# Whole 512-column units at the turn from pass 1 to pass 2 of a fused spectral and gated feed-forward kernel

## The chip, the cores and the metric

The kernel runs on one core of a Trainium2 chip. The metric is the device time of one execution in microseconds (us). Three runs of the kernel before took 1045.95 to 1046.25 us, with a median of 1046.12 us.

## The reference

Two layers, each of a spectral mixing with a residual and a feed-forward block with a residual, on x with 2048 rows and 512 columns:

```python
def _A_ref(x, w_r, w_i):                       # x: [1, 2048, 512]
    X = rfft2(x)
    X = X * (w_r + 1j * w_i)                   # [2048, 257]
    return irfft2(X, s=(2048, 512))

def _B_ref(x, w_gate, w_up, w_down):           # F = 1792
    g = einsum("bsd,df->bsf", x, w_gate)
    u = einsum("bsd,df->bsf", x, w_up)
    return einsum("bsf,fd->bsd", g * u, w_down)

for _ in range(2):
    x = x + _A_ref(_layernorm(x), w_r, w_i)
    x = x + _B_ref(_layernorm(x), w_gate, w_up, w_down)
```

All is in float32.

## The kernel before

**Layout.** The 2048 rows are 16 tiles of 128 (index t). Every layer has the transform stages (`fwd`, `middles`, `inv`) and then the feed-forward part. The feed-forward part takes F in 14 blocks of 128 features (`ft`) and runs twice over them: pass 1 for row tiles 0 to 7 (`h0 = 0`), pass 2 for tiles 8 to 15 (`h0 = 8`). Pass 1 goes through the blocks upward and pass 2 downward, so that the weights of the last blocks are still there. The place between the two passes is called the turn; there is one in each layer.

**A unit** (`unit`) computes g, u and g*u for one block of 128 features and one pass. It uses a 2 x 2 scheme with seven products instead of eight, so X is kept as seven *forms*, f0 to f6: `xA` holds f0, f1, f2 and `xS` holds f3 to f6, each as `[form, high or low, k, 512 columns]`. A form is a sum of blocks of X; its high part is a cast made by ScalarE (ACT) and its low part the difference to the full value, a subtraction made by GpSimd (POOL). A product is six matmuls (`mm3` for two k: high by high, high by low, low by high). In the order in which a unit uses them: gw on f3, gx on f1, gy on f4, gx on f2, gz on f5, gv on f6, gz on f0. A unit covers 512 columns (`half` is None), or a half unit covers 256 of them.

**The downs** bring g*u back to 512 columns. Layer 0's pass 1 does it directly (`db`, three 512-wide matmuls on tiles `wd` and `h`). The three other passes use the seven-product scheme again (`down`: `ex`, `ey`, `ew`, `ev`, `ez`, six 256-wide matmuls each), on forms `sf` of g*u, again a cast by ACT and a subtraction by POOL, and on forms `bf` of the down weights. Layer 0 makes these forms, stores them (`dn`), and loads them as `bf` for pass 2 and for layer 1. `bf` lies in the memory of `h` and `wd`, so the first of them can be loaded only behind the last `db` of pass 1.

**The second X.** `xA` and `xS` exist once. While pass 1 runs, the forms of pass 2's rows are prepared in a staged copy, the tile `xf`, `[4 row blocks r, 8 pieces, k, 128]` (`stage_x`): normalised rows are transposed through DRAM (`turns`), and POOL makes the sums. `unstage_x` (line 721) then copies them into `xA` and `xS`, for one row block r at a time: three casts by ACT (768, 512 and 512 columns) and three subtractions by POOL of the same widths. It is called for two row blocks at k = 16 of the main sequence and for the other two at k = 18. A copy must wait until the products of pass 1 that read its columns have run.

**What sets the order.** The main sequence `seq` lists the units. Around the turn it was: whole units up to block 11, then half units (12, 13, 12, 13 in pass 1; 13, 12, 13, 12 in pass 2), then whole units from block 11 down. Its index k also places the stages, the weight loads (`weights`, `kept_weights`) and the due times (`begins`). But the order of the instructions on each engine is a finished table: `Plan.order` reads `ORDER`, a compressed list of all operations of the program in the order of issue, and `PLACES`, which names the buffer of each tile. Each engine executes its instructions in that order. All are issued through one helper, so that the profile has one line for nearly all, L314 (`Queue.call`); they are told apart by the tiles' names. SyncE (SP) issues the DMAs.

Of the kernel before, what the change touches and what calls it, by code (L numbers as in the profile page):

```python
# [28 lines left out]
def consts():  # L29
# [86 lines left out]
    'c-lRh37n7B_s7qDW-&92F=mLdj2Zhr)<MaVeNBpFDYRNDm8C>zv4m2Qq<&Gf$d-MVtT7D3*mpk)5zP!^=DFwpzK{MtUcSro+~?f0e9k$abH79iit;B)ZfQ};(R*4zjAUssxvM$aPzuNa'  # L116
    '-XD@&J*Cl7LU!tda#KU(Ppu@|G)Y1wfhTkHA1%z9a;z>Xw>3t}$|a<hlw(>=3dvsNUC>0irbVQrM9F@x#>sYGlVq)?BH^CCEt~YL9?~-M2hY7GbM=JQk*jKv`nP6lAvE2`oh13MZbH`<'
    'a!4D=KkOAJH_+`U|9nlB6DHbLWX*XkA=!Ly#QsZJbynlJe^H;1^GHsVZ%j{n7dhqSH||6sqn@18)7l#At4JCv8?e_l{83mU*((;CqU4VLp*OXLT+~uX{|9{*XkWRkW#t=fj~$VC@3gj*'
    'UiuFECd&wYo-0>1A@D>jT2#ePxA4aSU95v;7W(|9t?*}zln;x`JECcL_+DU{Vo^4c31Mw7FU0QQdoirthi2#Wt`S=ec~L~A7#`LjayPZ0l*7Wx{M(@Qv7?TpYk9nWSqI>wOl+;f)5p+!'
    'mA)yv(X1R#89tT6z8G{oKwKY`m8|JQq}s|Jy^QYX^$ziAf}Eu~S|;mQaq-#7^JV3A?IBBamF&>lL^xKe$!ebI!tUF&BmOKZ(d<!@`>oL?PA2O6*q5*2_$V9Sox<;KuUJXsbAnXonO-uE'  # L120
    '7|hiX@~WN*-<f+&`%6QaLR{nVew4(6u%hy`t_E52Z3k0@?;~}tRAi^W_&ZYP5H0uZE)q}bE4n~Rf$Cha6e}+BcXfo0XHA?$fUvQ6>nmL^ZS_}auFK>XeOiu#gl2qpnGquy`jYODJniN!'
    '@Qd)iTOI-V&zWrdI~dL)I?js;nrL=wDZMOJiFpYvYNBPGz9n0bP)BBKNj)m<q^>NpSJ0{pIQ|?&wUc_}%_e(Hx|^SEJGo$+g{1p?^ny3pPvc1=Ps$f)_!)WD7lf_TDq6(cw5`p2ogs5{'
    'g;oH4ZKXdr>?yBkKVq4o=WKanvExattmTczlMA#Pk=mwT%0fNPZe64dE9Ynn*~-6CGD<hda6To;e~8Z`(nE&u-hw)CRp#4z(v&QHR?d6(@_Vt1uc7*o36%r3mT8BCwHhXcw754^U)81('
    '#+7;IE89(mT4UNsbJ;F&`n^6Ztz|4Za$RDH%#Ru>7D?gKU3!6z2~?NGVDJMpy>InK{Sj1bCF>W7hXr+AKFCz<jE6hubZM-!C5`V#L2+eJc|bQwD}4&7i$G{aDMH4$JBPI~Pv(+=A##M*'
    'AISJwGE{%ngLqA~J6d_fC=<l&(HHRFU1WvhgJ|ORv>ql#xAZH#QW34%;)!9%OC%#U>ML?kBjf>Dtk20OSh!P%@ccI2E^ksP7DyzL?_pVnyst0GcSw1Ty7CY8?hP=Lt5?yrF<JMXHs|$0'
    'RwPh$rh@(t@k2#y*$$>kn7g3AusPsYFs=p{lL5r3C4TnM@isVeahz|q+D*FEPB2@@*@L#Ec~(|n?=eaD8<|`QQ7cPBM&+H9)3yp8J*r8@w}m8EA~Z|GOg^8lkt5~gjFi`fwxJhE-tW*n'
    '`P<f&({j(om}D~co)pkO@$3V}uy&6vYS#JfyaTqO$)|pO4qC#&%VrHVp5{w^WOguXeZ{}k$=Rto9Di=r>MCZg|E{?pLXWA4{Nj3pI$&6nq6a|YaT{gwY?3K0SM;<^Hs>_gRyAkU+NNd~'
    'NchfHGV~W4XCm?W4f}{mCmW7xaV<>+z9c#J7P1;3bGbeWR`aQt*QqV>`1vCB<OV&*Ros<20klSG1UsFuC%D#KmXUL1Kwku}M$V9lE2%?2bLV#(Z?=*Pk>q3-d04)&E#-4+tI(<Hm^_`w'
    'y7Tr0JHl&4hs~!tAJd`!Chre+iUsFC+a4xSrrOud8`?kznf=5tLyuV_Pf!7jq?#u3G4I3h-WufAmf3i?HI=m{$SWuL_BlJtt10D(<`ytuWIa{*wk`oL>-8BrO9cKtL!2tmy(UW^`?z@;'
    'l#T%xe-gLFc8FQ4Ep;Uo>`Sc$#+KN>wY^!QFVj!9YgwYuMJC%(cv}3UUPrE7VTV;j?{BJ58mR3@CrJdW4}p%pGSH4OY5F*t46tL(Hgr%>U61FUk!S2eb3(_nq9YyuPd!IGE@&I_cR2|B'  # L130
    'UYk)1%gbBXJJ2{=dfO-&V^-657TO#zw#}^9_w6|Doxqb;Pm+Hz=<={s*0r*cI$cC+5TBED;j>6@DQmcv4Enm#VV3G;JJg)UYs>M@DRo@rq<&!MnLgCPM%1ULOm#ZJCOUfx{9`5^us>IS'
    '(hVk=`WQ++_r~+>>4Jx;J3Z|b6KA8nRr;+Bl?CP(n81Uwi<+|ljmjdkH#RH)e=V@>Nj{}YCHKj0HG}9Z4h_k62RVG0eBVbbhM5E@VI!$EQ%oh9Pha{5{OtE5yz1cQq^7dZCb=WeP<1;?'
    'Y3ZcPY`E9W9yZ7Prn1Ylx2H`8e$9oKm9hoB@_3~Zxae+=X_m<Zp>cMz?m~7eSWt}3)B|R)9c^0R&(2`F3_WF<yrs|EO{S2o<VD(DrjCT$z2<@r(2qc$YPKII`6d-R#$chZkv3I4bI?}y'
    'b`kv@n&l_b6@M@v$V7QUzrj<>k(glXd)NKWUT3g#%kLt&=<qH6Z$@RTCjEjQi`Q%p9sD@#Cl9oY^OL-Densz;-_u*|r+63XVJE22d;E#sd;a6zeCkn#pC1xu(~)S+UYP0;zle8*Sni_3'
    'td%K#H*cOFBXhj5pl6(X3Hw;-J7)BSw}M?J$QZp#7w_hU;HQaxb+BZlj(5iI=M|8j{dc`PdR&+IZ+XN0N4zEem!3g`v%WRCNInXKyr@I5pscjSb4f6sHU1*)h_+8q9m?{(CQm#gZ^LYN'
    'N?v|*&nG&q!1_PBoA>2Zx-k0J3OdIrD*sI#;_vYsW-^Vj&h}QYk{F(^CgY_;Xpg*8epT-yf1y`_Yrp$syEn`q><#vx@p?-ezdp}?fQEa?_Jw#TK`PMSd|1^FdQd0H*LZA<zDFHt>Gy%Z'
    'Z1xrg?63qKWUbEeYkQ4lnm@<;K^M?-9ss?LL6?W!FEgd=QU7W0Q}zgz5pcIfx`OID(qHZ!r>m4E$M(|gAB2B3@qhKsV%;Y4`3leHVdW@)ig$wVm+|Ke{5jF2<z4bFQwvX+_3*0eI+L!E'
    'fFCdG8-81_JdC^|ewph}BR28U-EZx^N8LKE)BWLI5==Hh8u_z=dvkTG{~PGIfu&FQC%kC?Z?B4f${U9l3dm^xq~}Qke<;4Z1{0|3pZBiAOY0-OINhKm9ki5xiHcmGoF73XO2UBp;jLJz'
    'M?8E*HQxW)OZDr@6(n6GpKs|FeGJ>qQ7K~3I4t0yu~NVf5829W&?}g8zSnA|87%)Q9w;r2y)BZ*bg6U%14;ChQuLn=#5@kW$}`uvPX^@16CcM~%E5GtP|HihCpyZ-{9nA5vXUxP3qCT2'
# [12 lines left out]
    '?kv}O_$5Ln>1*&NH=`DXRm}9Vbe8vtulWT-in0DV|0C~ld|g&*N?LvvJk32_Up^sP*~Dz98DcBK7H$&R45o#g{HvZrk~>8_s4u`?Zn2NAyFkx1`a^djasPDl0v44Amw)I_W~BAVu9E0<'
# [131 lines left out]
def kernel(ctx: ExitStack, tc: tile.TileContext, x, wf, wc, wb, dfwd, tf, ti, mid, out):  # L284
# [16 lines left out]
    def f32(ap):  # L301
        return ap.bitcast(F32)
# [888 lines left out]
```

## Time and profile before

| | |
|---|---|
| median of three runs | 1046.12 us |
| the profiled execution | 1047.8 us |
| its span | 1046.0 us |
| granted TensorE clock (mean) | 0.998 |
| layer 0's turn | about 286 to 345 us |
| layer 1's turn | about 801 to 858 us |

How to read the rows that are shown below: a row of the timeline has the start, the duration, the engine, the line, the operation, `out<-in`, the shape and how many such instructions ran in a row. A group has the count, the busy time in us and the mean of one in ns, then the idle time before it and what ended it. A stretch has the window, its length, then the busy time (and count) of PE, PEld, DVE, ACT and POOL, the granted clock, the share of the DMA engines and GB/s. A row on a wait has the waiting engine and tile, the engine and tile that ended the wait, the time in all, how often, and the longest. A matmul's duration overlaps that of the next one, since matmuls are pipelined; the distance of starts is what one takes.

### The profile page before, as it was taken

How to read it: one execution, taken by the hardware profiler on the slowest of the kernel's cores; microseconds unless marked ns; L12 is line 12 of the kernel's file. 1: busy time of each engine (PE TensorE's matmuls, PEld its weight loads, DVE VectorE, ACT ScalarE, POOL GpSimd, SP SyncE). 2: the span in 40 equal slices, each digit the busy share in tenths (PEclk: the TensorE clock that was granted, in tenths of full speed). 3: DMA queues.
4: the chain of work that ended last, by engine and by line, in shares of the span. 5: the costliest groups of instructions: out<-in, count | busy, mean ns of one | idle time of the engine just before them, and what ended most of it. 6: DMA issues, size and time to landing. Idle time of an engine off the chain costs nothing.

```text
span 1046.0 us, 19456 instructions
## 1 busy us (share of the span) xinstructions
PE 1028.3 (98%) x6884; PEld 898.9 (86%) x6884; DVE 803.7 (77%) x1581; ACT 421.3 (40%) x1011; POOL 748.4 (72%) x960
## 2 busy tenths in 40 slices
PE   8899999999999999999999999999999999999998
PEld 6676988888899888889987779888889998888897
DVE  7669867768877567778887697788888766767688
ACT  6568534343453232233366693223333421222231
POOL 6868899999999644666789367555578964536671
PEclk9999999999999999999999999999999999999999
DMA  9525256668773854646372005455787266464642
GB/s 359 226 84 183 73 207 231 235 219 272 245 231 134 284 194 160 218 145 231 142 293 104 7 11 202 153 177 176 194 274 219 91 221 214 170 210 171 223 142 81
DMA packets 129473, 193.71 MB, mean 185 GB/s; under 512 B 39265, under 2 KB 50785, under 8 KB 127329
## 3 DMA queue, kind: packets, MB, share of 16 engines
q1 hardware_dynamic: 129088, 191.95, 54.0%
q8 instruction: 55, 0.90, 0.3%
q10 hardware_dynamic: 288, 0.52, 0.1%
q14 instruction: 42, 0.34, 0.1%
HBM read 145.52 MB, written 46.92 MB: 184 GB/s over the span
## 4 chain that ended last, share of the span: by engine, by line
PE 86%; DVE 5%; POOL 4%; issue 1%; ACT 0%; DVEq 0%; POOLq 0%; ACTq 0%
PE gz L314 15%; PE gx L314 15%; PE db L314 8%; PE gy L314 7%; PE gw L314 7%; PE gv L314 7%; PE ex L314 5%; PE ez L314 5%; PE ey L314 3%; PE ew L314 3%; PE ev L314 3%; DVE xs L314 2%; PE vq L314 2%; POOL fs L314 2%; PE yi L314 2%; PE dp L314 1%
## 5 line engine op out<-in xcount | busy, mean ns | idle before, releaser
L314 PE MATMUL gx<-xA,wt 128*128 128x512 f32 (+1 forms) x852 | 179.3, 346 | 0.0
L314 PEld LDWEIGHTS gx<-xA,wt 128*128 128x128 f32 x852 | 137.9, 189 | 17.9
L314 POOL TENSOR_TENSOR sf<-q,sf 128x256 fp32r<-128x256 f32 x99 | 73.3, 746 | 106.4 <-ACT sf L314 97.3
L314 POOL TENSOR_TENSOR sf<-cc,sf 128x256 fp32r<-128x256 f32 x97 | 72.0, 745 | 55.5 <-ACT sf L314 48.7
L314 DVE TENSOR_TENSOR xs<-xs,db 128x512 f32<-128x512 f32 x128 | 85.5, 681 | 23.3 <-PE db L314 22.7
L314 PE MATMUL db<-wd,h 128*128 128x512 f32 x336 | 91.3, 392 | 0.1
L314 PE MATMUL gy<-xS,wt 128*128 128x512 f32 (+1 forms) x426 | 89.9, 346 | 0.0
L314 PE MATMUL gz<-xS,wt 128*128 128x512 f32 (+1 forms) x426 | 89.8, 346 | 0.0
L314 PE MATMUL gz<-xA,wt 128*128 128x512 f32 (+1 forms) x426 | 89.6, 346 | 0.0
L314 PE MATMUL gw<-xS,wt 128*128 128x512 f32 (+1 forms) x426 | 89.6, 346 | 0.0
L314 PE MATMUL gv<-xS,wt 128*128 128x512 f32 (+1 forms) x426 | 89.4, 345 | 0.0
L314 ACT COPY s<-gx 128x512 f32<-128x512 f32 (+1 forms) x71 | 35.2, 496 | 130.9 <-PE gx L314 130.5
L314 PEld LDWEIGHTS gz<-xS,wt 128*128 128x128 f32 x426 | 69.0, 189 | 9.5 <-DVE q L314 0.5
L314 PEld LDWEIGHTS gw<-xS,wt 128*128 128x128 f32 x426 | 69.1, 189 | 9.1
L314 PEld LDWEIGHTS gz<-xA,wt 128*128 128x128 f32 x426 | 69.0, 189 | 9.0
L314 PEld LDWEIGHTS gv<-xS,wt 128*128 128x128 f32 x426 | 69.0, 189 | 9.0
L314 PEld LDWEIGHTS gy<-xS,wt 128*128 128x128 f32 x426 | 68.6, 190 | 8.6
L314 DVE TENSOR_TENSOR q<-gy,s 128x512 f32<-128x512 f32 (+1 forms) x71 | 41.0, 577 | 45.2 <-PE gy L314 32.9
L314 ACT CAST sf<-q 128x256 fp32r<-128x256 f32 x99 | 40.0, 407 | 82.1 <-DVE q L314 41.7
L314 PEld LDWEIGHTS db<-wd,h 128*128 128x128 f32 x336 | 61.1, 188 | 11.8 <-POOL h L314 0.4
L314 POOL TENSOR_TENSOR wt<-rg,wt 128x512 fp32r<-128x512 f32 (+1 forms) x56 | 64.3, 1159 | 4.3 <-ACT wt L314 4.2
L314 PE MATMUL ex<-bf,sf 128*128 128x256 f32 x396 | 58.1, 283 | 0.0
(166 smaller groups left out, 2505.9 us busy)
## 6 DMA issues: line engine op xcount, KB each, us to landing
wt<-gu SPq DMA_DIRECT2D x36, 1024.0 KB, 6.9
wt<-gu SPq DMA_DIRECT2D x36, 768.0 KB, 6.7
bf<-dn SPq DMA_DIRECT2D x20, 1024.0 KB, 5.5
wq<-in_wf_dram SPq DMA_DIRECT2D x16, 1024.0 KB, 8.6
bf<-dn SPq DMA_DIRECT2D x20, 768.0 KB, 4.6
gu<-wt SPq DMA_DIRECT2D x14, 1024.0 KB, 5.5
gu<-wt SPq DMA_DIRECT2D x14, 768.0 KB, 5.3
rg<-in_wb_dram SPq DMA_DIRECT2D x14, 512.0 KB, 3.8
```

The lines of the kernel that those rows point to most:

```text
L314: ins = f(*args, **kw)
```

## The change

The half units at the turn become whole ones: blocks 12 and 13 are done like all others, with 512 columns, in both passes. (The half units at the beginning of pass 1 and at the end of pass 2 stay.) `unstage_x` is called once per layer, at k = 16, and goes form by form: f3, f1, f4, f2, f5, f6, f0, in which a form is one cast of 1024 columns by ACT and one subtraction of 1024 columns by POOL (all four row blocks, both k). The indices in the main loop move by the four entries that `seq` loses before the end and the two before the turn. `ORDER` and `PLACES` are new, for the whole program.

```diff
 ORDER = (
-    'c-lRh37n7B_s7qDW-&92F=mLdj2Zhr)<MaVeNBpFDYRNDm8C>zv4m2Qq<&Gf$d-MVtT7D3*mpk)5zP!^=DFwpzK{MtUcSro+~?f0e9k$abH79iit;B)ZfQ};(R*4zjAUssxvM$aPzuNa'
+    'c-l=`2Y6LgwqE<(n+ha>fE1A?y%<W6lA(nzRWv9?1yM$w!4XlB0VAS<qBx9guopxf3r!_b9s~ucf=UZD2#Pdm34w%r_Im$Xdx!TvzH@WVKD(^G{<RK7QHrC=bdIm5Gi=D<+0Y5@K&5<<E0T;'
...
-    def unstage_x(X, st, nm):
+    def unstage_x(X, st):
         XA, XS = X
-        r = nm.ts[0] % 4
-        cols = slice(128 * r, 128 * r + 128)
-        s = lambda i, j: st()[:, r, i:j]
-        act(768, lambda: A.copy(XA()[:, :, 0, :, cols], s(1, 4)), [(st, i, r) for i in (1, 2, 3)], [(XA, i, 0, r) for i in range(3)])
-        for h in (0, 2):
-            act(512, lambda h=h: A.copy(XS()[:, h:h + 2, 0, :, cols], s(4 + h, 6 + h)), [(st, 4 + h, r), (st, 5 + h, r)],
-                [(XS, h, 0, r), (XS, h + 1, 0, r)])
-        lows = (dve, tt, 900, dict(two=True)) if LOWS == "DVE" else (pool, gtt, 768, {})
-        lows[0](lows[2], lambda: lows[1](XA()[:, :, 1, :, cols], s(1, 4), f32(XA()[:, :, 0, :, cols]), ALU.subtract),
-                [(st, i, r) for i in (1, 2, 3)] + [(XA, i, 0, r) for i in range(3)], [(XA, i, 1, r) for i in range(3)], **lows[3])
-        for h in (0, 2):
-            pool(512, lambda h=h: gtt(XS()[:, h:h + 2, 1, :, cols], s(4 + h, 6 + h), f32(XS()[:, h:h + 2, 0, :, cols]),
-                                      ALU.subtract),
-                 [(st, 4 + h, r), (st, 5 + h, r), (XS, h, 0, r), (XS, h + 1, 0, r)], [(XS, h, 1, r), (XS, h + 1, 1, r)])
+        for b in (3, 1, 4, 2, 5, 6, 0):
+            t, i = (XA, b) if b < 3 else (XS, b - 3)
+            src = lambda b=b: st()[:, :, b + 1].rearrange("p r k s -> p k r s")
+            at = lambda hl, t=t, i=i: t()[:, i, hl].rearrange("p k (r s) -> p k r s", r=4)
+            rs = range(4)
+            act(1024, lambda src=src, at=at: A.copy(at(0), src()), [(st, b + 1, r) for r in rs], [(t, i, 0, r) for r in rs])
+            pool(1024, lambda src=src, at=at: gtt(at(1), src(), f32(at(0)), ALU.subtract),
+                 [(st, b + 1, r) for r in rs] + [(t, i, 0, r) for r in rs], [(t, i, 1, r) for r in rs])
...
-        seq = [(0, 0, 0), (1, 0, 0), (0, 1, 0), (1, 1, 0), *((ft, None, 0) for ft in range(2, 12)), (12, 0, 0), (13, 0, 0),
-               (12, 1, 0), (13, 1, 0), (13, 0, 8), (12, 0, 8), (13, 1, 8), (12, 1, 8), *((ft, None, 8) for ft in range(11, 1, -1)),
+        seq = [(0, 0, 0), (1, 0, 0), (0, 1, 0), (1, 1, 0), *((ft, None, 0) for ft in range(2, 14)), *((ft, None, 8) for ft in range(13, 1, -1)),
...
-            u = UNITS[layer][k >= 18]
+            u = UNITS[layer][k >= 16]
...
             if k == 16:
-                for ts in pairs[4:6]:
-                    unstage_x(X, stage, nms[ts[0]])
-            if k == 18:
-                for ts in pairs[6:]:
-                    unstage_x(X, stage, nms[ts[0]])
-            if k == 22 and layer == 0:
+                unstage_x(X, stage)
+            if k == 18 and layer == 0:
...
-            i = 2 * layer + (k >= 18)
-            if k in (0, 18):
+            i = 2 * layer + (k >= 16)
+            if k in (0, 16):
...
-            if (4 <= k < 16 or 22 <= k < 34) :
+            if 4 <= k < 16 or 18 <= k < 30:
                 ws[ft] = weights(ft, begins[k] + STO) if i == 0 else kept_weights(ft)
```

What the new table does at the turns is seen in the rows of each engine's program.

TensorE at layer 1's turn, before: pass 1 ends with a half unit of block 13, and pass 2 begins with one of block 13. `gx<-xA` is a product on f1 or f2, `gz<-xA` one on f0, `gz<-xS` one on f5; `ex` to `ev` are downs.

```order
L314 MATMUL gz<-xA,wt 128x256 x6
L314 MATMUL gx<-xA,wt 128x256 x6
L314 MATMUL ew<-bf,sf 128x256 x6
L314 MATMUL ev<-bf,sf 128x256 x6
L314 MATMUL gx<-xA,wt 128x256 x6
L314 MATMUL gy<-xS,wt 128x256 x6
L314 MATMUL gw<-xS,wt 128x256 x6
L314 MATMUL ez<-bf 128x256 x6
L314 MATMUL gz<-xS,wt 128x256 x6
L314 MATMUL gv<-xS,wt 128x256 x6
L314 MATMUL gx<-xA,wt 128x256 x6
```

The same place of the change, from the last product of pass 1 on f6 (`gv`) to the first two of pass 2 on f1 and f2:

```order
L301 MATMUL gv<-xS,wt 128x512 x6
L301 MATMUL gx<-xA,wt 128x512 x6
L301 MATMUL ez<-bf,sf 128x256 x6
L301 MATMUL gz<-xA,wt 128x512 x6
L301 MATMUL ez<-bf,sf 128x256 x6
L301 MATMUL gx<-xA,wt 128x512 x6
L301 MATMUL ex<-bf,sf 128x256 x6
L301 MATMUL gx<-xA,wt 128x512 x6
L301 MATMUL ex<-bf 128x256 x6
```

All products are 512 wide now, there are half as many of them, and a form's last product of pass 1 (f2 and f0 here) stands only a few rows ahead of the first of pass 2.

GpSimd at layer 1's turn, before (`xA<-xf` and `xS<-xf` are low parts of the second X, `xf<-xf` its staged sums, `sf`, `bf`, `cc`, `q` and `s` belong to the downs' forms):

```order
L314 TENSOR_TENSOR xS<-xf,xS 128x2x2x128
L314 TENSOR_TENSOR sf<-cc,sf 128x256
L314 TENSOR_TENSOR cc<-cc 128x256
L314 TENSOR_TENSOR bf<-s_9473,bf 128x256
L314 TENSOR_TENSOR xf<-xf 128x256
L314 TENSOR_TENSOR xA<-xf,xA 128x3x2x128
L314 TENSOR_TENSOR sf<-cc,sf 128x256
L314 TENSOR_TENSOR sf<-q,sf 128x256
L314 TENSOR_TENSOR xA<-xf,xA 128x3x2x128
L314 TENSOR_TENSOR cc<-cc,q_9556 128x256
L314 TENSOR_TENSOR sf<-cc,sf 128x256
```

And of the change, from f1's low part on:

```order
L301 TENSOR_TENSOR xA<-xf,xA 128x1024
L301 TENSOR_TENSOR sf<-s_9231,sf 128x256
L301 TENSOR_TENSOR xS<-xf,xS 128x1024
L301 TENSOR_TENSOR sf<-cc,sf 128x256
L301 TENSOR_TENSOR bf<-q,bf 128x256
L301 TENSOR_TENSOR xS<-xf,xS 128x1024
L301 TENSOR_TENSOR sf<-cc,sf 128x256
L301 TENSOR_TENSOR sf<-q,sf 128x256
L301 TENSOR_TENSOR sf<-cc,sf 128x256
L301 TENSOR_TENSOR cc<-cc 128x256
L301 TENSOR_TENSOR s_9451<-q_9375,cc 128x256
L301 TENSOR_TENSOR xA<-xf,xA 128x1024
```

Before, low parts of one row block stand in turn with staged sums of the next one; now the staged sums are all ahead of the first low part, and whole forms of 1024 columns alternate with the downs' forms.

GpSimd at layer 0's turn, of the change (`h` is the low part of g*u for `db`, `wd` that of down weights, `rw` and `u_` are sums of down weights whose stores the load of `bf` waits for, `fo` belongs to the next layer's transform):

```order
L301 TENSOR_TENSOR xA<-xf,xA 128x1024
L301 TENSOR_TENSOR h<-q,h 128x512
L301 TENSOR_TENSOR wd<-rw,wd 128x512
L301 TENSOR_TENSOR xf<-xf 128x256 x5
L301 TENSOR_TENSOR xS<-xf,xS 128x1024
L301 TENSOR_TENSOR h<-q_3607,h 128x512
L301 TENSOR_TENSOR xA<-xf,xA 128x1024
L301 TENSOR_TENSOR xS<-xf,xS 128x1024
...
L301 TENSOR_TENSOR xS<-xf,xS 128x1024 x2
L301 TENSOR_TENSOR fo<-xs 128x256 x2
L301 TENSOR_TENSOR rw<-rw 128x256
L301 TENSOR_TENSOR xA<-xf,xA 128x1024
L301 TENSOR_TENSOR rw<-rw 128x256 x4
L301 TENSOR_TENSOR u_3848<-rw,u_3848 128x256
```

The seven low parts stand between those of h; the last of them, f0, stands ahead of the sums of weights.

159 lines of the change are left out of this document (73 added, 86 removed).

## The prediction

> **What bounds the kernel now.** I read the page's head first, then the groups of instructions with different shapes kept apart, then the timeline of single engines and the busy time by stretches around the two turns.
>
> ```profile
> span 1046.0 us, 19456 instructions
> PE 1028.3 (98%) x6884; PEld 898.9 (86%) x6884; DVE 803.7 (77%) x1581; ACT 421.3 (40%) x1011; POOL 748.4 (72%) x960
> POOL 6868899999999644666789367555578964536671
> PE 86%; DVE 5%; POOL 4%; issue 1%; ACT 0%; DVEq 0%; POOLq 0%; ACTq 0%
> PE dp L314 <- DVE fs L314: 3.1, 3, 1.7
> PE tq L314 <- ACT xn L314: 1.8, 3, 1.0
> ```
>
> TensorE is busy for 98% of the span and holds 86% of the chain that ended last. The two longest of its waits (dp, tq) lie in the transform stages; no wait for a form of X is in that list. So at the turns the time is the number of matmuls times their spacing, and the only other engine near its limit is GpSimd, whose digits stand at 9 over a quarter of the span. Now the turns, by stretches (layer 0: first two rows; layer 1: fourth):
>
> ```profile
> core 0: us, PE busy (x) PEld busy (x) DVE busy (x) ACT busy (x) POOL busy (x), PEclk, DMA share, GB/s
> 250.00:286.60 36.60, 36.60 (x163) 30.28 (x162) 31.49 (x64) 14.47 (x29) 36.13 (x38) 1.00 0.74 242
> 286.60:345.00 58.40, 58.37 (x417) 54.53 (x416) 42.08 (x95) 25.11 (x59) 57.77 (x64) 1.00 0.61 194
> 346.00:400.00 54.00, 54.00 (x292) 46.72 (x291) 36.14 (x58) 14.34 (x39) 27.38 (x39) 1.00 0.63 225
> 806.20:846.60 40.40, 40.40 (x339) 40.36 (x338) 32.75 (x65) 16.93 (x39) 39.88 (x46) 1.00 0.33 101
> ```
>
> At both turns TensorE and GpSimd are full together: 58.37 and 57.77 of 58.4 us, 40.40 and 39.88 of 40.4. Right behind layer 0's turn GpSimd is half idle (27.38 of 54). Neither engine waits for the other now, but TensorE cannot get shorter at a turn by more than GpSimd can follow. That is the whole question. The granted clock is 1.00 in all rows, so it plays no part.
>
> **What the wide products save.** A matmul's own duration is a modelled end and overlaps the next, so I take the spacing of groups of six (one product), start to start.
>
> ```profile
> 269.62 1.52 PE L314 MATMUL gw<-xS,wt 128*128 128x512 f32 x6
> 270.98 0.84 PE L314 MATMUL db<-wd,h 128*128 128x512 f32 x3
> ...
> 774.91 1.55 PE L314 MATMUL gx<-xA,wt 128*128 128x512 f32 x6
> 776.30 0.88 PE L314 MATMUL ew<-bf,sf 128*128 128x256 f32 x6
> 777.01 0.88 PE L314 MATMUL ev<-bf 128*128 128x256 f32 x6
> ...
> 838.45 0.88 PE L314 MATMUL gz<-xS,wt 128*128 128x256 f32 x6
> ...
> 842.05 0.88 PE L314 MATMUL gz<-xA,wt 128*128 128x256 f32 x6
> ...
> L314 PE MATMUL gx<-xA,wt 128*128 128x256 f32 x360 | 53.2, 284 | 0.0
> ```
>
> Six 256-wide matmuls take 0.72 us (838.45 to 842.05 is five groups, 3.60). Six 512-wide take 1.36 beside 512-wide ones (269.62 to 270.98); behind a 256-wide group they take 1.39, and that narrow group then 0.71 (774.91 to 777.01), so about 1.38 net. A pair of half products costs 1.44, the whole product that replaces it 1.37 on average: 0.07 saved. The change turns 16 half units into 8 whole ones (blocks 12 and 13, two passes, two layers), 7 products each, 56 pairs: 56 x 0.07 = **-3.9 us**. Its ends are 56 x 0.05 = 2.8 (all at 1.39) and 56 x 0.08 = 4.5 (all at 1.36). The number of columns stays the same; what goes is 336 instructions' fixed share.
>
> That row can be set beside a rule. The Trainium skill, page "TensorE: Matmul & The Clock Gate", section "Back-to-back issue gap", gives the warm isolated gap as N/2.4 + 2.5 ns. By it a pair would save six times 2.5 ns, 0.015 us, and the whole change an estimated 0.8 us. The rows above disagree: 120 ns and 227 to 232 ns for one, so that two narrow ones cost 8 to 13 ns more than a wide one. The measurement decides here.
>
> DVE and ACT also do fewer, wider instructions in those units. Every one of them is now hidden behind TensorE (32.75 and 16.93 of 40.4 us above), and less work there hides as well: 0, and nothing to lose from it.
>
> **What the second X costs GpSimd.** Its low parts are brought in whole forms, 1024 columns per instruction, seven per turn, instead of four times (768 + 512 + 512).
>
> ```profile
> L314 POOL TENSOR_TENSOR sf<-q,sf 128x256 fp32r<-128x256 f32 x99 | 73.3, 746 | 106.4 <-ACT sf L314 97.3 <-PE ev L314 9.0
> L314 POOL TENSOR_TENSOR xS<-xf,xS 128x512 fp32r<-128x512 f32 x16 | 20.6, 1298 | 0.0
> L314 POOL TENSOR_TENSOR xA<-xf,xA 128x768 fp32r<-128x768 f32 x8 | 14.9, 1857 | 0.0
> 835.67 1.86 POOL L314 TENSOR_TENSOR xA<-xf,xA 128x768 fp32r<-128x768 f32 x1
> 837.48 0.75 POOL L314 TENSOR_TENSOR bf<-cc,bf 128x256 fp32r<-128x256 f32 x1
> 838.18 0.76 POOL L314 TENSOR_TENSOR sf<-q,sf 128x256 fp32r<-128x256 f32 x1
> 838.88 1.87 POOL L314 TENSOR_TENSOR xA<-xf,xA 128x768 fp32r<-128x768 f32 x1
> ...
> 842.10 1.31 POOL L314 TENSOR_TENSOR xS<-xf,xS 128x512 fp32r<-128x512 f32 x1
> 843.35 0.76 POOL L314 TENSOR_TENSOR xf<-xf 128x256 f32<-128x256 f32 x1
> ```
>
> Durations grow by 552 and 559 ns per 256 columns, so 1024 columns should take 2.41 us. Back to back, the next starts 0.05 earlier than the end: 0.70 for 256, 1.25 for 512, 1.81 for 768, hence 2.36 for 1024. No row shows that width. It lies between 1.86 (the 768 row) and 2.98 (four 256 rows); I take 2.36, nearest to the 768 row and on the line through three. A turn's low parts then need 7 x 2.36 = 16.5 us, before 4 x (1.81 + 2 x 1.25) = 17.2. The copies of ACT go by the same line (621 and 835 ns for 512 and 768 columns):
>
> ```profile
> L314 ACT CAST xS<-xf 128x512 fp32r<-128x512 f32 x16 | 9.5, 621 | 11.9 <-POOL xf L314 11.9
> L314 ACT CAST xA<-xf 128x768 fp32r<-128x768 f32 x8 | 6.5, 835 | 3.4 <-PE gz L314 3.4
> ```
>
> That is 1.05 us for 1024 (0.84 to 1.24 by these rows), on an engine that is 42% busy there.
>
> The total is no problem; the deadlines are. X is single-buffered: a form's copy starts when the last product of pass 1 that reads it has ended, and its low part must be there before the first product of pass 2.
>
> *Layer 1.* By the new order TensorE has, from the start of pass 1's last gw on f3 to pass 2's first gz on f0, 15 products and 21 downs: 15 x 1.37 + 21 x 0.72 = 35.7 us. GpSimd's row in the same stretch begins with f1's low part. f1 is free after two products (2.74), its copy is done 1.05 and a handover of 0.1 later: 3.9. From there to the end of f0's low part stand 7 wide and 23 narrow ones: 7 x 2.36 + 23 x 0.70 = 32.6. A saturated GpSimd also loses a little between instructions (0.52 of 40.40 us in the row above), 0.6 with a handover to TensorE of 0.1 behind it. So f0 is ready at 3.9 + 32.6 + 0.7 = 37.2, and TensorE waits **+1.5 us** in all. By the same count f5 and f6, which GpSimd brings shortly ahead of f0, are already 0.3 and 0.6 late, so the wait should show there first. Price ends: with 1024 columns at 1.86 nothing is left of it (0); at 2.98 it is 1.5 + 7 x 0.62 = 5.8. GpSimd is free enough behind the turn that the wait isn't passed on.
>
> *Layer 0.* There the same seven low parts stand among the low parts of h and of the last down weights. Counting the rows of both orders, f6 and f0 come 0.2 to 0.7 us before they are needed. Behind them four narrow sums of weights and eight rows more must end before the stores of the last down forms, and the load of all forms comes last:
>
> ```profile
> 331.05 0.37 SPq L314 DMA_DIRECT2D bf<-dn  x1
> ...
> 339.25 0.88 PE L314 MATMUL ex<-bf,sf 128*128 128x256 f32 x6
> bf<-dn SPq DMA_DIRECT2D x20, 1024.0 KB, 5.5
> ```
>
> Before, the load was issued at 331.05 and the first ex ran at 339.25, 8.2 us later, with 5.5 us for a load: 2.7 us of slack. With 2 us less of TensorE (half of the saving) and an order that leaves GpSimd no gap, I count 0 to 2 us of slack and take **+0.4** (0 to 2.7). The SP queue issues nothing more than before; the load waits behind the same stores.
>
> **The rest.** The table of orders is new for the whole program, so stalls in the transform stages can move both ways; the longest now is 1.7 us, and I take 0 with 1.5 to either side. The sum against the profiled execution (span 1046.0, own time 1047.8) is -3.9 + 1.5 + 0.4 = -2.0, so 1045.8; the median of the runs shown is 1046.12, 1.7 below, and gives **1044.1**.
>
> **Rivals.**
> 1. GpSimd hides everything. For it: low parts shrink by 0.7 us a turn, and a price of 2.15 instead of 2.36 would be enough at layer 1. Against: 39.88 of 40.40 us are taken. Then all 3.9 us stay: 1042.2.
> 2. Layer 0's handover takes the place of the wait removed. GpSimd's row there ends later than counted, and every microsecond goes through the stores and the 5.5 us load to the first ex. At 2 us more than I took (the far end of the slack) the sum is 0: 1046.1. A second place with the same price is the staged tile at layer 1: a whole form needs all four row blocks, where a row block was brought for itself before, and the last two loads take 4.1 us each:
>
> ```profile
> DMA to landing us min/median/max: 2.6/4.1/6.9
> ```
>
> The new order puts the last sums of that tile ahead of f1's low part on GpSimd; where they come 2 us late, all behind them does, and the sum is 0 again.
> 3. Slower: the wide low part is the bound. Its operands are runs of 128 columns out of four row blocks; if those cost as four narrow instructions, 0.62 us more each, layer 1 waits 4.3 more, and layer 0, whose slack is used up, 4.3 more: -2.0 + 8.7 = +6.7, 1052.8. The change turns slower than before at an excess of 0.14 us each (14 x 0.14 = 2.0), and measurably from 0.29, a spacing of 2.65. Against it: the 512 and 768 rows also write runs of 128 columns and lie on the line.
> 4. The change does not do what it says: the fixed share of a narrow matmul is hidden at the turn and a pair costs what a whole product does. Then 0 + 1.5 + 0.4 = +1.9, 1048.0, inside what counts as no change. The pitches of 0.72 and 1.37 speak against it. The rule of the Trainium skill weighed above ("TensorE: Matmul & The Clock Gate") would end near here, an estimated 0.8 us lower.
>
> **How the numbers follow.** Forecast 0.58, rival 1 0.18, rival 2 0.14, rival 3 0.06, rival 4 0.04. A measurement of this kernel can tell about 0.2% (2.1 us) from no change: 1044.0 and 1048.2. The forecast lies on the first bound; with the spread of its terms (2.8 to 4.5, 0 to 3, 0 to 1) I give it 0.27 faster and 0.31 within. With rival 1 faster has 0.45; rival 3 and the worse tail of 2 give slower 0.09; the rest, 0.46, is no change that can be told. The range, 1041.5 to 1047.3, leaves out rivals 3 and 4, a gain of the new order on top of rival 1, and the worst of rival 2, under 0.2 together.
>
> **What would show it.** In the profile of after, the 256-wide gx group should fall from 360 to 168 (14 half units are left of 30) and no product be narrower at the turns; the low parts should show about 2.41 us; TensorE's waits at layer 1's turn (800 to 860) should name GpSimd and f5, f6, f0, 1.5 us in all; at layer 0 the first ex should stand within 0.5 us of the matmul ahead of it. The prediction is wrong if a low part takes over 2.6 us, if TensorE shows no wait at layer 1, or if the stretches outside the feed-forward part differ by over 1.5 us.

## The result, and the profile after

| | before | after |
|---|---|---|
| median, same chip | 1046.18 us (6 runs, 1045.81 to 1047.21) | 1056.85 us (6 runs, 1053.36 to 1062.03) |
| ratio | | 1.0103, 95% interval 1.0072 to 1.0133 |
| profiled execution, span | 1047.8, 1046.0 us | 1053.65, 1051.9 us |

The change makes the kernel slower, by 10.7 us between the medians, and its runs lie 8.7 us apart where those of before lie 1.4 apart. The forecast was 1044.1, the range 1041.5 to 1047.3. The profiled execution of after is one of its two fastest, so the profile shows only 5.9 us of the loss.

The head of the page of after, answering to the lines shown of before:

```profile
span 1051.9 us, 18665 instructions
...
PE 1028.2 (98%) x6548; PEld 882.9 (84%) x6548; DVE 797.0 (76%) x1525; ACT 419.2 (40%) x989; POOL 746.6 (71%) x946
...
PE 85%; DVE 7%; DMA 4%; POOL 2%; issue 1%; ACT 1%; SPq 1%; DVEq 0%; POOLq 0%; ACTq 0%
```

Matmuls went from 6884 to 6548, the 336 that the change takes out. The shares by engine look alike. What is new stands in the chain of work that ended last: DMA holds 4% of it, and before it held none. TensorE's waits say the same (waiting engine and tile, what it waited for, us in all, times, longest):

```profile
PE tp L301 <- POOL fo L301: 2.3, 1, 2.3
PE dp L301 <- DVE fs L301: 2.1, 3, 1.6
PE gz L301 <- DVE q L301: 1.9, 1, 1.9
PE ev L301 <- DMA bf<-dn: 1.3, 1, 1.3
...
PE gz L301 <- DMA wt<-gu: 1.1, 1, 1.1
```

Three of these rows lie in the feed-forward part (both `gz`, and `ev`), two of them name a load. The low parts of the second X, on which the prediction's +1.5 us rested, are in none of these rows. (The whole list has one row in which TensorE waits for a low part, 0.4 us at 630 us; that is layer 1's first X.)

The stretches that were shown of before (window, length, busy time and count of PE, PEld, DVE, ACT, POOL, then granted clock, DMA share, GB/s):

```profile
250.00:286.60 36.60, 36.60 (x163) 30.17 (x162) 31.04 (x63) 14.64 (x29) 36.13 (x39) 1.00 0.76 230
286.60:345.00 58.40, 56.55 (x254) 46.63 (x253) 37.50 (x64) 21.66 (x41) 50.63 (x48) 1.00 0.66 208
346.00:400.00 54.00, 54.00 (x303) 47.19 (x302) 37.59 (x61) 17.75 (x48) 31.51 (x45) 1.00 0.62 217
806.20:846.60 40.40, 38.45 (x226) 33.20 (x225) 29.23 (x44) 16.83 (x32) 38.27 (x38) 1.00 0.27 87
```

At the turns TensorE now stands still for 1.85 and 1.95 us, and GpSimd is *less* busy than before (50.63 after 57.77, 38.27 after 39.88). So neither of the two bounds the turn any more. Where does the time go? For every matmul I took the distance to the next start and subtracted what the same shape takes undisturbed (227 ns with 512 columns, 120 with 256, and so on for the shapes of the transform stages). Summed by stretch this is TensorE's loss in us; the rest of the span is the matmuls themselves.

| loss in | 0 to 120 | to 280 | to 520 | to 640 | to 760 | to 860 | to the end | all | matmuls |
|---|---|---|---|---|---|---|---|---|---|
| before | 14.5 | 0.0 | 1.7 | 6.8 | 0.7 | 0.3 | 0.9 | 24.9 | 1021.1 |
| after | 13.4 | 0.1 | 4.7 | 9.0 | 0.8 | 4.1 | 2.7 | 34.7 | 1017.2 |
| after, again (e0_again) | 13.1 | 1.6 | 5.5 | 9.4 | 0.8 | 6.5 | 3.1 | 40.1 | 1017.1 |

The matmuls became 4.0 us shorter, as forecast (-3.9). The loss grew by 9.9 us in one execution and by 15.2 in another, in four places: both turns and what follows them (280 to 520 and 760 to 860), the start of layer 1 (520 to 640), and the end.

Now one loss closely. At layer 1's turn of after, TensorE (start, duration, engine, line, operation, tiles, shape, count, and in brackets the idle time before it and what ended it), then the chain over the same stretch (start, us, what):

```profile
806.18 1.55 PE L301 MATMUL gx<-xA,wt 128*128 128x512 f32 x6
809.06 0.95 PE L301 MATMUL ev<-bf,sf 128*128 128x256 f32 x6 [1.34 <-DMA bf<-dn]
```

```profile
795.61 3.87 DMA turns<-zt
...
799.50 0.34 SPq L301
...
799.89 0.70 SPq L301
...
800.69 0.43 SPq L301
801.12 0.04 issue
801.16 7.77 DMA bf<-dn
808.93 0.14 issue
809.06 0.95 PE ev L301 x6
```

Read it from the bottom. The `ev` should have begun at 806.18 + 1.38 = 807.56 and began at 809.06, 1.5 us late (the row's 1.34 is less, because a matmul's modelled end lies behind the next one's start), when the load of its form block landed (801.16 + 7.77 = 808.93). The load was not late because it was slow alone: it was issued late. Its buffer came free at 797.58, but the queue of SyncE stood at a reload of staged rows (`xf`, issued 799.50) that waited for a staging store to land (795.61 + 3.87). A load of weights (799.89) and the second reload (800.69) came next. Before, the same load went out at once, ahead of the staging stores and with both reloads ten us behind it:

```profile
796.17 0.42 SPq L314 DMA_DIRECT2D bf<-dn  x1
796.64 8.18 SPq L314 DMA_DIRECT2D turns<-zt  x6
806.55 0.34 SPq L314 DMA_DIRECT2D xf<-turns  x1
```

and it landed after 5.6 us, 2.1 us before it was needed. In after it was in flight beside the reloads, and took 7.8. The other places have the same form. In layer 0's second pass a load of 1 MB of weights stood behind a form block's load and then took 9.73 us (439.87 to 449.60; TensorE lost 1.3). At layer 0's turn it is one step removed. ScalarE waits for raw weights,

```profile
290.20 0.92 ACT L301 CAST wt<-rg 128x256 fp32r<-128x256 f32 x2 [2.83 <-DMA turns<-zt]
291.03 0.58 ACT L301 COPY s<-gx 128x512 f32<-128x512 f32 x1
```

and the copy that `gz` needs by way of VectorE stands in order behind that cast. (The row names a staging store, which is where the profile puts the last event; the cast reads `rg`, whose load was issued at 284.14 and landed at 290.12.) That is the 1.9 us of `gz <- DVE q`. Together the waits that lead back to a landing at 292, 450, 798, 809, 865 and 1019 us cost 2.0 + 1.3 + 0.3 + 1.5 + 0.4 + 0.4 = 5.9 of the 9.9 us.

Loads were little slower on the whole: the median from issue to landing went from 5.5 to 5.7 us for form blocks of 1 MB and from 4.6 to 5.1 for those of 768 KB, and the bytes are the same. But more of them land late. Of the 231 loads, 35 instead of 21 land less than 0.5 us ahead of their first use, counted from the program's dependences and the landings in the two traces. Among the 112 loads of form blocks and unit weights, for which TensorE stands directly, it is 8 instead of 1.

### The profile page after: what moved, and what is told of

The parts are those of the page before. It is cut to its first block, busy times and chain, and to the rows that moved or that the text cites. A ratio compares the mean times of both kernels' runs of the same rounds, so it can differ in the third digit from the quotient of the medians.

```text
span 1051.9 us, 18665 instructions
## 1 busy us (share of the span) xinstructions
PE 1028.2 (98%) x6548; PEld 882.9 (84%) x6548; DVE 797.0 (76%) x1525; ACT 419.2 (40%) x989; POOL 746.6 (71%) x946
## 4 chain that ended last, share of the span: by engine, by line
PE 85%; DVE 7%; DMA 4%; POOL 2%; issue 1%; ACT 1%; SPq 1%; DVEq 0%; POOLq 0%; ACTq 0%
PE gz L301 13%; PE gx L301 13%; PE db L301 7%; PE gv L301 7%; PE gw L301 7%; PE gy L301 7%; PE ez L301 5%; PE ex L301 5%; DVE xs L301 3%; PE ew L301 3%; PE ev L301 3%; PE dp L301 2%; PE tp L301 2%; PE zp L301 2%; PE ey L301 2%; PE vq L301 2%
## 5 line engine op out<-in xcount | busy, mean ns | idle before, releaser
L301 PE MATMUL gx<-xA,wt 128*128 128x512 f32 (+1 forms) x756 | 176.5, 368 | 0.7 <-DVE mv L301 0.3
L301 PEld LDWEIGHTS gx<-xA,wt 128*128 128x128 f32 x756 | 129.7, 189 | 22.2 <-ACT s L301 0.6
L301 PEld LDWEIGHTS gz<-xS,wt 128*128 128x128 f32 x378 | 64.6, 189 | 13.9 <-DVE q L301 2.3
L301 PEld LDWEIGHTS gw<-xS,wt 128*128 128x128 f32 x378 | 65.0, 189 | 12.4 <-POOL xS L301 1.4
L301 PEld LDWEIGHTS gz<-xA,wt 128*128 128x128 f32 x378 | 64.9, 189 | 10.4
L301 PEld LDWEIGHTS db<-wd,h 128*128 128x128 f32 x336 | 62.2, 188 | 13.4 <-DVE sx L301 0.5
L301 PEld LDWEIGHTS gv<-xS,wt 128*128 128x128 f32 x378 | 64.8, 189 | 10.3
L301 PEld LDWEIGHTS gy<-xS,wt 128*128 128x128 f32 x378 | 64.2, 189 | 10.0 <-DVE cc L301 0.3
L301 ACT CAST sf<-cc 128x256 fp32r<-128x256 f32 x98 | 39.7, 406 | 62.0 <-PE ew L301 15.4
```

What stands on the lines that cost most here:

```text
L301: ins = f(*args, **kw)
```

## The experiments

Two theories. **D**: TensorE stands where loads land late, because the new table has the DMA queue issue them later or beside other transfers. **G**: the wide low parts on GpSimd are the bound at the turns, as the +1.5 us and the third rival of the prediction have it. Medians are compared with those of before on the same chip (1045.9 to 1047.2).

**The change again.** No edit.

> The changed kernel once more, for a second profile of it and for its spread. Theory D (late landings): the time lost lies where an engine waits for a DMA that landed late, so the places and sizes of TensorE's waits differ between two profiles of the same program, by 1 to 5 us in all, while the sum of its matmuls stays within 0.3 us; 1053 to 1060 us. Theory G (GpSimd's wide low parts hold TensorE at the turns, as the prediction had it): the waits are the same in both profiles, within 0.5 us.

1057.59 us (4 runs, 1054.15 to 1058.96), ratio 1.0098 (1.0078 to 1.0119). The loss repeats. Its profile (1058.96 us) shows other places than the first (1053.65 us; third row of the table above):

```profile
PE ev L301 <- DMA bf<-dn: 2.2, 2, 1.5
PE ex L301 <- DMA bf<-dn: 2.1, 2, 1.6
...
PE gz L301 <- DMA wt<-gu: 0.5, 1, 0.5
```

Four waits for form blocks where the first profile has one of note, and less for `wt`. What stays the same is the kind. A load with a few tenths of slack is late in one execution and in time in the next. That is one way in which the runs come to lie apart; only two executions of after were profiled. Another is in the same profile: the wait at 292 us (`gz <- DVE q`, 1.9 us in both) is followed here, and not in the first profile, by 3.4 us at a granted clock of 0.50, which cost 1.6 us more (the last section has the rows).

**Eight instructions moved.** Six are DMA issues (two loads of weights at 440 us go ahead of the form block's load, and four issues at layer 1's turn change places so that the form block's load goes ahead of the reloads). Two are on ScalarE: the copy at 291 us and what TensorE needs at 865 go ahead of a cast that waits for a load:

```diff
+MOVES = ((1627, 1661), (2284, 2161), (2285, 2161), (4029, 3464), (3907, 3902), (3468, 3902), (4030, 3478), (4773, 4239))
...
+        turn = [int(i) for i in turn]
+        for a, b in MOVES:
+            turn.remove(a)
+            turn.insert(turn.index(b), a)
```

> The changed kernel with eight entries of its order moved, so that nothing on TensorE's path waits for the five late landings of its profile: the copy of gx at 290 us goes ahead of two casts of raw weights, the two weight loads of 434 and 440 us are issued some 15 us earlier, at layer 1's turn one weight load goes ahead of the turn stores, the load of bf ahead of two loads of the staged X and one weight load behind them, and at 863 us a cast of raw down weights goes behind a copy. Theory D: the waits at 292 (2.0), 449 (1.25), 809 (1.5) and 864 us (0.35) go, 5 us in all; profile 1048 to 1050 us against 1053.7, and the spread of the runs falls to about half of 9 us. Theory G: no change beyond 1 us, since no low part of X moves.

1050.77 us (9 runs, 1048.79 to 1055.26), ratio 1.0048 (1.0034 to 1.0062): 6.8 us less than e0_again with no matmul, cast or low part changed. The waits at 292, 450, 809 and 865 us are gone, and TensorE's loss falls to 31.3 us. That speaks for D. The runs still lie 6.5 us apart, where about half of 9 was expected. Waits for loads are left at 795 and 1016 us.

**Low parts a quarter as wide.** The low parts of three of the four row blocks of the second X are left out, so that GpSimd has 7 x 1.67 = 11.7 us less at each turn:

```diff
-            pool(1024, lambda src=src, at=at: gtt(at(1), src(), f32(at(0)), ALU.subtract),
+            pool(1024, lambda src=src, at=at: gtt(at(1)[:, :, 0:1], src()[:, :, 0:1], f32(at(0))[:, :, 0:1], ALU.subtract),
```

> The changed kernel with the low parts of the second X made for 256 of 1024 columns only (the other columns are left as they were); GpSimd is relieved by 7 x 1.66 = 11.6 us at each turn, and nothing else changes. Theory G: faster by 1.5 us or more, TensorE's waits at the two turns fall by that. Theory D: the landings stay late, within 1 us of the changed kernel's fast runs, the same waits at 292, 449 and 809 us.

1055.92 us (4 runs, 1055.10 to 1057.48), ratio 1.0085 (1.0068 to 1.0102), which overlaps e0_again's. GpSimd's low parts and TensorE's waits:

```profile
L301 POOL TENSOR_TENSOR xS<-xf,xS 128x256 fp32r<-128x256 f32 x8 | 5.8, 738 | 0.2 <-ACT xS L301 0.2
L301 POOL TENSOR_TENSOR xA<-xf,xA 128x256 fp32r<-128x256 f32 x6 | 4.4, 738 | 1.2 <-ACT xA L301 1.2
```

```profile
PE gz L301 <- DMA wt<-gu: 2.0, 1, 2.0
PE ev L301 <- DMA bf<-dn: 1.8, 1, 1.8
```

Twelve us less on GpSimd at each turn bring 1.7 us between the medians. G asked for 1.5 or more, so the time alone does not decide: the intervals overlap, and 1.7 would also meet it. The waits decide. The two for loads stay, and from 812 to 850 us, where the low parts of layer 1's second X stand, TensorE's loss is 2.0 us here and 2.0 in after. As the cause of the loss G falls: in after, GpSimd is not what TensorE waits for.

**The products in halves.** In blocks 12 and 13 each product is done as two of 256 columns, in the order of after. (As written, the sums of these products come out changed; the number and the shape of the matmuls are what is tested.)

```diff
-                for k in range(2):
-                    mm3(p(o), w[:, 0, wn, k], w[:, 1, wn, k], xt()[:, i, 0, k, cols], xt()[:, i, 1, k, cols],
-                        start and k == 0, stop and k == 1)
+                for c in (slice(0, 256), slice(256, 512)) if ft in (12, 13) else (cols,):
+                    for k in range(2):
+                        mm3(o()[:, c] if ft in (12, 13) else p(o), w[:, 0, wn, k], w[:, 1, wn, k], xt()[:, i, 0, k, c],
+                            xt()[:, i, 1, k, c], start and k == 0, stop and k == 1)
```

> The changed kernel with each product of blocks 12 and 13 (512 columns) issued as twice 256 columns, in the same place of the order: 336 matmuls more, the columns the same. If the prediction's first term is right, TensorE's matmuls take 3.9 us more (2.8 to 4.5); the time grows by 2 to 4 us, less than that where the loads that were late gain the time back. If the fixed share is hidden (rival 4), the matmuls take under 1 us more.

1060.29 us (4 runs, 1058.02 to 1062.37), ratio 1.0129 (1.0111 to 1.0147), 2.7 us above e0_again between the medians, with intervals that touch. The matmuls themselves are clearer: the 256-wide `gx` are back at 360, and the sum of the matmuls is 1021.4 us, 4.2 above after. The saving of the wide products is real and independent of the order.

**The mirror: the kernel before with three late loads.** The raw weights of 286 us, the form block of 449 and that of 802 are issued later in the queue of *before*; no unit is wide.

```diff
+MOVES = ((3985, 4057), (2240, 2236), (1652, 1560))
```

> The kernel before, with three loads issued later in the DMA queue and nothing else moved: the raw weights that landed at 286.22 us (behind four more issues, about 2.4 us later), the weights of the form block that landed at 448.56 (behind one load of 1 MB, landing near 451.7 where 449.5 is needed), and those that landed at 801.81 (issued near 803, landing near 809 where 803.9 is needed). Theory D: TensorE gains waits of about 2, 2 and 5 us at these three places and the time rises by 6 to 10 us, to 1052 to 1056, without any wide form. Theory G: the kernel before has cover for them, 1046.5 plus or minus 1.5.

1056.35 us (5 runs, 1055.12 to 1057.79), ratio 1.0089 (1.0075 to 1.0103). Three late loads alone can cost 9.1 us, nearly as much as the change's 10.7. It is no measure of what each place costs in after, for the sizes differ: the third place costs 6.8 us here and 1.5 there. TensorE around it:

```profile
805.54 0.88 PE L320 MATMUL ew<-bf,sf 128*128 128x256 f32 x6
810.45 1.62 PE L320 MATMUL ev<-bf,sf 128*128 128x256 f32 x6 [4.03 <-DMA bf<-dn]
811.87 1.48 PE L320 MATMUL gz<-xS,wt 128*128 128x256 f32 x6
...
816.61 0.88 PE L320 MATMUL gz<-xA,wt 128*128 128x256 f32 x6
```

The wait is 4.2 us, and the five groups behind it take 6.2 us (810.45 to 816.61) instead of 3.6, so the late load costs 6.8 us there. That second part was not in the expectation; it is taken up at the end. The loss of its profile is 34.0 us, 9.1 more than before, of which 6.7 lie between 760 and 860 us.

**More slack for the loads: a first try.** e1_moves, with 299 places of the DMA queue's order changed; the compute engines keep theirs.

> The kernel after with the eight moves of e1_moves and the order of the DMA queue's own issues changed at 299 of its places, so that loads stand further ahead of their first use; the orders of the four compute engines are those of e1_moves. Theory D (TensorE stands where loads land late): the waits left in e1_moves at about 775, 795 and 1016 us go or shrink below 0.3 us, the time falls from 1050.8 to about 1048.0 (1046.5 to 1049.5), and the runs lie within 4 us instead of 6.5. Theory G (the wide low parts on GpSimd): no issue of a load matters, 1050.8 plus or minus 1.

1058.01 us (5 runs, 1054.17 to 1058.75), ratio 1.0097 (1.0080 to 1.0113): a miss, 7 us *slower* than e1_moves.

```profile
PE ex L298 <- DMA bf<-dn: 6.2, 3, 5.0
PE ev L298 <- DMA bf<-dn: 2.4, 1, 2.4
```

The time moves by 7 us with the issues alone, which is against G. But loads that had been in time are late: the form block needed at 767.6 us could have been issued at 760.8, stood behind a reload that waited for its stores and behind five more transfers, went out at 764.65 and landed at 772.62. I had reckoned the landings from bytes in flight, and the queue stopped at places that this reckoning did not have.

**A rule instead.** e1_moves again, with 25 moves in the DMA queue by one rule: what has long been ready goes ahead of the form block's load that it stood behind, what is needed late goes behind it.

> e1_moves with 25 further moves among the DMA queue's own issues (the four compute engines keep their orders): a load or store that had been ready for over 3 us but stood behind a form block's load, and was issued with it, now goes ahead of that load, and one whose use is over 10 us off goes behind it; four output stores that were issued beside the loads at 983, 984, 1002 and 1010 us go to 937 and 957. Theory D (landings): the form blocks that landed just as they were needed in e1_moves (at 767.7, 795.1 and 1015.6 us) land at least 0.8 us earlier, the waits of 0.74 and 1.42 us behind two of them go, and the time falls from 1050.8 to about 1048.0 (1046.5 to 1049.5), with the runs within 4.5 us instead of 6.5. If e5_loads failed for another reason than the places where it put these loads, 1050 or more. Theory G (low parts): 1050.8 plus or minus 1.

1049.72 us (9 runs, 1047.94 to 1052.30), ratio 1.0029 (1.0019 to 1.0039). Less than e1_moves by 1.05 us where 2.8 were expected; the runs lie 4.4 us apart, as expected. The wait at 1016 us went. At 796 us TensorE still stands, for 1.7 us. (The profile names a sum of VectorE there, which ended within 0.1 us of the landing. In e8_sp below, with VectorE's order the same, the `ex` starts at once, so it was the load.)

**That place alone.** In a run of nine issues of the queue, at 782 to 798 us, six change places: the form block's load goes ahead of staging stores and of one load of 768 KB. In the order of the queue, e6_prio to e7_sp:

```diff
-DMA wt<-gu_98 128x3x512
-DMA turns_15_121<-zt 128x4x32
 DMA bf<-dn_105 128x4x512
-DMA turns_15_121<-zt 128x4x32 x3
 DMA bf<-dn_105 128x3x512
+DMA turns_15_121<-zt 128x4x32 x4
 DMA xf<-turns_15_121 128x512
 DMA xf<-turns_11_122 128x512
+DMA wt<-gu_98 128x3x512
```

> e6_prio with ten places of the DMA queue at 782 to 798 us re-ordered: the load of the form block that landed at 796.08 where 794.5 was needed goes ahead of four staging stores and of a 768 KB weight load that were in flight beside it; the compute engines keep their orders. Theory D (landings): that load lands near 794, the wait of 1.69 us falls below 0.3 us, and the time falls from 1049.7 to about 1048.4 (1047.5 to 1049.5). Against D: no change of the wait, or the same time lost at the next load.

1053.80 us (5 runs, 1052.66 to 1054.65), ratio 1.0073 (1.0059 to 1.0087): 4 us slower instead of 1.3 faster. The wait at 796 us is gone, the loss from 780 to 800 fell from 1.9 to 0.1 us. It came back at the load that had been moved. TensorE and the DMA queue:

```profile
805.79 0.87 PE L298 MATMUL ev<-bf,sf 128*128 128x256 f32 x6
809.59 1.63 PE L298 MATMUL gw<-xS,wt 128*128 128x512 f32 x6 [2.92 <-DMA wt<-gu]
```

```profile
796.68 2.67 SPq L298 DMA_DIRECT2D turns<-zt  x4
802.48 0.81 SPq L298 DMA_DIRECT2D xf<-turns  x2
803.34 0.96 SPq L298 DMA_DIRECT2D wt<-gu  x2
```

After the four stores the queue stands for 3 us, until the last has landed and `xf` may be read, and the weights behind it go out at 803.34. I had counted on their slack, over 10 us, and not on what they would be queued behind.

**The orders of the compute engines too.** e7_sp, with the engines' orders changed in four stretches.

> e7_sp with the orders of the compute engines changed in four short stretches (316 to 334, 598 to 645, 775 to 815 and 990 to 1047 us), where e6_prio still had TensorE wait for results of VectorE, ScalarE and GpSimd in the new order (0.91 us at 328, 0.49 to 0.79 three times at 620 to 627, 0.5 at 1025). If what is left of the loss is the new order of the engines there, the time falls by about 0.6, 0.7, 0.2 and 1.2 us more, to 1046.0 (1045 to 1047.5), the time of the kernel before. If it is something that all the wide units share, it stays at that of e7_sp.

1057.62 us (4 runs, 1056.68 to 1058.88), ratio 1.0109 (1.0095 to 1.0122): a miss. The loss from 600 to 620 us rose from 4.1 to 8.8: its profile has one new wait there, of 3.0 us at 606 us, for VectorE's `rs`, with a granted clock of 0.50 for 6.8 us behind it. In that profile the miss comes from the order of this try. That the rest of the loss is the order of the compute engines is neither shown nor excluded by it.

**The moved load put right.** e7_sp, with the load of 768 KB ahead of the staging stores, and one reload ahead of the next form block:

```diff
 DMA wt<-gu_97 128x4x512
+DMA wt<-gu_98 128x3x512
 DMA turns_11_122<-zt 128x4x32 x3
 DMA bf<-dn_105 128x4x512
+DMA xf<-turns_11_122 128x512
 DMA bf<-dn_105 128x3x512
 DMA turns_15_121<-zt 128x4x32 x4
 DMA xf<-turns_15_121 128x512
-DMA xf<-turns_11_122 128x512
-DMA wt<-gu_98 128x3x512
```

> e7_sp with the 768 KB weight load that landed late in it (issued 803.34, landed 809.45, behind two reloads of staged rows that waited for their stores) issued near 784 us, ahead of three staging stores, and one staged reload issued before 796 us; nothing else moved. Theory D (landings): the wait of 3.07 us at 809 goes, the wait at 795 stays away, and the time falls from 1053.8 to about 1048.5 (1047.5 to 1049.5), a little below e6_prio. Against D: a fall of less than 2 us.

1049.98 us (9 runs, 1048.72 to 1052.28), ratio 1.0035 (1.0025 to 1.0045): 3.8 us faster than e7_sp by moving two transfers. Its TensorE shows neither the wait at 796 nor the one at 809 us. But it is not below e6_prio (1049.72). TensorE now waits for GpSimd behind that place. GpSimd, then TensorE:

```profile
802.88 0.74 POOL L298 TENSOR_TENSOR xf<-xf 128x256 f32<-128x256 f32 x1 [2.25 <-DMA xf<-turns]
810.10 2.40 POOL L298 TENSOR_TENSOR xA<-xf,xA 128x1024 fp32r<-128x1024 f32 x1
```

```profile
816.34 0.74 PE L298 MATMUL ew<-bf,sf 128*128 128x256 f32 x4 [0.73 <-POOL sf L298]
```

GpSimd stood for 2.25 us until the reload of staged rows had landed, so the sums of the staged rows come late and everything behind them too. The low part of f1 begins 5.9 us after the start of the last `gw` on f3 (804.18), where the prediction reckoned 3.9 (4.1 in after). A low part of a form for the down products, `sf` at 815.54, stands behind two wide low parts and ends at 816.28, and for that one TensorE waits, about 1 us. This is a wait for late staged rows, the second place of the prediction's second rival. No version that was run is faster than the kernel before.

What stays open: e8_sp's profile has 29.6 us of loss, 4.7 more than before: 3.7 more between 760 and 860 us, 1.6 at the start of layer 1 and 1.0 behind 860, less 2.0 at the program's start. What TensorE waits for there are VectorE, ScalarE and GpSimd in the new order. Their orders were tried only in e7_all, which made them worse. Whether the whole units can be brought below 1046 us in another order was not settled.

## Why the prediction was wrong

By its own steps:

**"-3.9 us" for the wide products: right.** The profile's groups, and TensorE's sum of 1017.2 after 1021.1 us (-4.0), with e3_halves as the cross-check (+4.2):

```profile
L301 PE MATMUL gx<-xA,wt 128*128 128x512 f32 x588 | 151.0, 392 | 0.2 <-ACT s L301 0.2
...
L301 PE MATMUL gx<-xA,wt 128*128 128x256 f32 x168 | 25.5, 285 | 0.5 <-DVE mv L301 0.3
```

The 256-wide `gx` fell from 360 to 168, as the prediction says. Its fourth rival (a pair costs what a whole product does) is out.

**"+1.5 us" for the second X on GpSimd: did not appear.** The price was right, 2.41 us for 1024 columns, forecast from the line through three widths:

```profile
L301 POOL TENSOR_TENSOR xS<-xf,xS 128x1024 fp32r<-128x1024 f32 x8 | 19.2, 2415 | 0.0
L301 POOL TENSOR_TENSOR xA<-xf,xA 128x1024 fp32r<-128x1024 f32 x6 | 14.5, 2410 | 1.2 <-ACT xA L301 1.2
```

and the third rival (up to 2.98) is out with it. The deadline moved. GpSimd's part, from the start of pass 1's last `gw` on f3 at 809.85 to the end of f0's low part at 846.74, took 36.9 us, where 37.1 was reckoned. But the same stretch of TensorE, reckoned at 35.7, took 37.3, since TensorE lost 1.1 us in it to waits for sums of VectorE, at a product (`gy`, 816 us) and at two downs (833 and 837 us):

```profile
844.34 2.40 POOL L301 TENSOR_TENSOR xA<-xf,xA 128x1024 fp32r<-128x1024 f32 x1
```

```profile
846.46 0.88 PE L301 MATMUL ev<-bf,sf 128*128 128x256 f32 x6
847.17 1.55 PE L301 MATMUL gz<-xA,wt 128*128 128x512 f32 x6
```

f0 came 0.43 us early, f5 and f6 0.9 and 0.7. The two engines are as close as I had counted, but TensorE's other waits let GpSimd get ahead. They do so also where the turn's waits for loads are gone: the same stretch took 37.4 us in e1_moves (805.80 to 843.19) and in e6_prio (806.76 to 844.11), and f0 is 0.5 us early in both. So no run shows this term as a wait. What was mis-sized in it is TensorE's own stretch, 35.7 reckoned and 37.3 to 37.4 measured; GpSimd's part came out. The first rival, that GpSimd hides everything, was right about this term, but not by its condition of a price of 2.15. e8_sp's wait at 816 us is not this term either: it comes from the late staged rows.

**"+0.4 us" for layer 0's handover: right within its ends.** The first `ex` follows at 348.52 on the group of 347.17, without a wait. I had feared the stores; the load landed 1.1 us ahead.

**The failed step is "The rest ... I take 0 with 1.5 to either side", and with it "The SP queue issues nothing more than before; the load waits behind the same stores."** It should have been about +10 to +15 us of loss (9.9 in one profile, 15.2 in the other). Both sentences look at *what* is issued. The table also changed *when* each load is issued and *behind what*: reloads of staged rows moved ahead of a form block's load, and loads of weights came to lie beside others. A form block's load took 4.3 to 11.0 us in these profiles, and many are needed soon after they land, so two us of delay in the queue can become a wait of TensorE. e1_moves got 6.8 us back by moving eight instructions, and m_late lost 9.1 us by moving three in the kernel before. The second place of the second rival (the staged tile at layer 1) was near it: the staged rows do decide that turn. But in after it is not their sums that come late; their reloads hold up the queue for a load that has nothing to do with them. (In e8_sp the sums come late too.)

The rows to see this were at hand. Before has 2.1 us of slack at the load of 796.17, and only two rows of it were read (`ex` of layer 0, and the landings of `xf`); the queue's order of before and of the change, one beside the other, was not read at layer 1's turn.

About 2.2 us of the loss lie at the start of layer 1 (520 to 640 us), with waits for VectorE, ScalarE and GpSimd rather than for loads. That is the "stalls in the transform stages" of the same sentence, beyond its 1.5.

## What to carry to other kernels

When a change brings a new order for a whole program, read the DMA queue's order first, load by load: when its buffer is free, what it stands behind, how long it takes beside what is in flight, and when it is needed. In the kernel before, 18 of the 112 loads of form blocks and unit weights land less than 2 us ahead of their first use, and TensorE waits for none of them; in after it is 27, with 6 of them under 0.2 us or late. Landings of the same kind of load vary by more than 2 us. So a new order can lose there what the arithmetic saves, and here it lost more. And put a wait for a store's landing (a reload through DRAM) behind the urgent loads of the same queue, never ahead of them.

## What was not expected of the hardware

**A wait can cost more than its length.** In m_late, behind the wait of 4.2 us, the stretches show the granted clock (the third number from the end):

```profile
810.40:814.40 4.00, 3.95 (x18) 3.98 (x19) 1.72 (x3) 0.41 (x1) 1.46 (x2) 0.50 0.37 82
814.40:816.50 2.10, 2.10 (x14) 2.10 (x13) 0.85 (x2) 0.00 (x0) 0.00 (x0) 0.59 0.43 43
816.50:822.00 5.50, 5.50 (x48) 5.50 (x47) 4.19 (x8) 4.08 (x9) 4.61 (x5) 1.00 0.12 42
```

It is 0.50 up to 816.1, 6.8 us from 809.3 on, and then TensorE is back at its pace. In e5_loads, behind its wait of 5.0 us, it is 0.50 for 3.4 us, and in e7_all, behind one of 3.0, for 6.8. Behind the wait of 2.9 us in e7_sp the groups keep their pace (1.46 us for six of 512 columns, then 1.38), and behind those of 2.0 us in after and in e3_halves too. But a wait of 1.9 us in e0_again has a slow stretch behind it:

```profile
293.58 1.80 PE L301 MATMUL gz<-xS,wt 128*128 128x512 f32 x6 [1.76 <-DVE q L301]
294.90:298.30 3.40, 3.40 (x10) 2.62 (x9) 1.24 (x3) 1.75 (x3) 3.32 (x5) 0.50 1.07 283
```

The Trainium skill, page "TensorE: Matmul & The Clock Gate", section "Part 1: The HAM clock gate (the "warmup" mystery)", has the clock fall to half after an idle window of about 3.4 us and rise after as long a busy one. The slow stretches of 3.4 and 6.8 us fit one and two such windows. The fall behind a wait of 1.9 us does not fit, and the measurement decides. So the length of a single wait does not tell what it costs: 4.2 us cost 6.8 in m_late, and 1.9 us cost about 3.5 in e0_again. What else decides it, no run here settles.

**Landings vary.** The 40 loads of form blocks took 4.4 to 9.1 us in after (median 5.4) and 4.3 to 11.0 in before. That before has the longer worst case and no wait shows that the slack at each load counts, not the worst landing.
